# Softmax sums on VectorE in place of ones matmuls, in an attention and FFN block on one core

## The chip, the cores and the metric

The kernel runs on one NeuronCore of one Trainium2 chip. The metric is the device time of one execution in microseconds (us); lower is better.

The engines in question: TensorE (PE in the profile; PEld is its weight load), VectorE (DVE), ScalarE (ACT), and SyncE (SP), whose instruction queue issues nearly all DMA transfers of this kernel. PSUM holds the tiles that TensorE's matmuls write in this kernel (names ending in `_ps`); an "eviction" is the copy or addition by which VectorE or ScalarE empties a PSUM tile.

## The reference, cut to what matters

```python
# x: 1 x 2048 x 1024, 32 query heads of 128, 4 key/value heads, window W = 512, all bf16
mod = (_silu(c) @ w_mod).reshape(c.shape[0], 6, 1, -1)       # sa, ca, ga, sb, cb, gb
h = _layernorm(x) * (1 + ca) + sa
# attention:
q = (x @ wq).reshape(B, Sq, Hq, Dh).transpose(0, 2, 1, 3)    # x is h here
k = jnp.repeat(k_cache[:, :, Sk - W:, :], rep, axis=1)       # v alike
scores = jnp.einsum('bhqd,bhkd->bhqk', q, k) * Dh ** (-0.5)
p = _softmax(scores, axis=-1)
o = jnp.einsum('bhqk,bhkd->bhqd', p, v)
#   ... o @ wo
x = x + ga * attention(h)
h = _layernorm(x) * (1 + cb) + sb
x = x + gb * ((_silu(h @ w_gate) * (h @ w_up)) @ w_down)     # the FFN, 3584 wide
```

The kernel computes `exp(scores)` without subtracting a maximum (it proves a bound on the scores while it runs), so each softmax needs the sum of 512 exponentials per query and head, its reciprocal, and a multiplication of `o` by that reciprocal.

## The kernel before

One step `k` of the attention loop handles one of 128 units: a head of a chunk of 512 tokens, 4 x 32. The exponentials `pT` lie with the keys on the partitions (4 tiles of 128 keys) and the 512 queries along the row. So the sum over keys is a sum over 4 tiles, which VectorE does (`psA`, `psB`), and then a sum over 128 partitions. Before, TensorE did the latter with a matmul against a matrix of ones, once for four heads (`l_ps`), and ScalarE made the reciprocal as `exp(-ln(sum))`. The reciprocals go through DRAM (`r_d`) and come back copied to all partitions (`rb`).

```python
    def mm(name, ...):                        # q_ps, o_ps, a_ps, l_ps share four PSUM tiles
        return psp.tile(list(shape), dt, name=name, tag="mm", bufs=4)
    def fetch(out, in_):                      # every load goes through SyncE, in this order
        pin(nc.sync.dma_start(out=out, in_=in_), "dma")
    ...
    def ln_stats(tt, late=None):              # LayerNorm statistics of 128 tokens
        ...                                   # two bn_stats on VectorE
        nc.vector.bn_aggr(out=mv[:, 0:2], in_=st)
        nc.scalar.activation(out=mv[:, 2:3], in_=mv[:, 1:2], func=ACT.Ln, bias=eps_t)
        nc.scalar.activation(out=mv[:, 2:3], in_=mv[:, 2:3], func=ACT.Exp, scale=-0.5)
    ...
    def put_q(g, q_ps):
        t = wk.tile([P, TCW], BF16, name="qT", tag="row", bufs=5)
        nc.vector.tensor_copy(out=t, in_=q_ps)
    ...
    def emit_s(g):
        ...                                   # 4 s_ps matmuls, 2 exponentials of 128x1024
        nc.vector.tensor_tensor(out=a, in0=p[:, 0:2, :], in1=p[:, 2:4, :], op=ALU.add)   # psA
        b = wk.tile([P, TCW], BF16, name="psB", tag="psB", bufs=5)
        nc.vector.tensor_tensor(out=b, in0=a[:, 0, :], in1=a[:, 1, :], op=ALU.add)
        rec[g] = b

    def emit_l(g):                            # once for four heads
        l_ps = mm("l_ps")
        for i in range(4):
            nc.tensor.matmul(l_ps[32 * i:32 * i + 32, :], lhsT=ones_bf[:, 0:32],
                             rhs=rec.pop(g - 3 + i), start=True, stop=True)
        r = wk.tile([P, TCW], FP32, name="rinv", tag="f32", bufs=2)
        nc.scalar.activation(out=r, in_=l_ps, func=ACT.Ln)
        nc.scalar.activation(out=r, in_=r, func=ACT.Exp, scale=-1.0)
        d = dp.tile([4, TCW], FP32, name="r_d", tag="r_d", bufs=4)
        nc.scalar.dma_start(out=d, in_=r[0:P:32, :])          # written from ScalarE's queue
        rinv[g // 4] = d
    # load_rb: two fetches of r_d, spread to 128 partitions; emit_norm: oT *= rb on VectorE
    ...
    def emit_wo(cc, q, u):                    # output projection: 8 a_ps matmuls, 4 rounds q
        ...
        if q == 0:
            nc.vector.tensor_copy(out=acc[(cc, t)][:, dsl], in_=a_ps)
        elif q < NQ - 1:
            nc.vector.tensor_tensor(out=acc[(cc, t)][:, dsl], in0=a_ps, in1=acc[...], op=ALU.add)
        ...                                   # last round: f, gate, residual
    ...
    for k in range(NU + 1):
        if k % 4 >= 2 and 4 * (k // 4) + 8 < NU:
            g = 4 * (k // 4) + 8
            load_wq(g // H, (g % H) // 4, (k % 4 - 2,))       # one of two tiles of next wq
        if k < NU:
            emit_s(k)
        if k + LEAD < NU:
            emit_q(k + LEAD)                                  # 8 q_ps matmuls, then put_q
        ...
        run_tasks(k)                                          # wo, rb, norm, LayerNorm, loads
        if k >= 1:
            if k % 4 == 0:
                emit_l(k - 1)
            emit_o(k - 1)                                     # 4 o_ps matmuls, copy by ScalarE
```

A scheduler orders the instructions of TensorE, VectorE and ScalarE, apart from those that `pin` keeps in program order. Any edit can therefore shift instructions elsewhere, and single microseconds are approximate.

Of the kernel before, what the change touches and what calls it, by code (L numbers as in the profile page):

```python
# [8 lines left out]
ACT = mybir.ActivationFunctionType  # L9
ALU = mybir.AluOpType  # L10
AX = mybir.AxisListType
BF16 = mybir.dt.bfloat16
FP32 = mybir.dt.float32
# [575 lines left out]
def fast_path(ctx, tc, flag, A_x, A_k_cache, A_v_cache, A_wq, A_wo, B_x, B_w_gate, B_w_up,  # L589
# [3 lines left out]
    nc = tc.nc  # L593
    P = 128
    _, S, D = A_x.shape
# [7 lines left out]
    TCW = 512  # L603
# [9 lines left out]
    scale = float(Dh) ** -0.5  # L613
# [15 lines left out]
    const = ctx.enter_context(tc.tile_pool(name="const", bufs=1))  # L629
# [5 lines left out]
    wk = ctx.enter_context(tc.tile_pool(name="work", bufs=2))  # L635
# [4 lines left out]
    def blkA(name, shape, dt=BF16):  # L640
        return pa_.tile(shape, dt, name=name, tag="A")

    def blkB(name, shape, dt=BF16):
        return pb_.tile(shape, dt, name=name, tag="B")
# [4 lines left out]
    def mm(name, shape=(P, 512), dt=FP32):  # L649
        return psp.tile(list(shape), dt, name=name, tag="mm", bufs=4)  # L650

    def big(name, shape=(P, 2, 512), dt=FP32):
        return psp.tile(list(shape), dt, name=name, tag="s", bufs=2)
# [6 lines left out]
    def pin(ins, what="steps"):  # L660
        return tc.keep_in_program_order(ins) if stage[what] else ins

    def fetch(out, in_):
        pin(nc.sync.dma_start(out=out, in_=in_), "dma")  # L664

    def load(out, in_):
        with nc.allow_non_contiguous_dma(reason="weight slice"):
            fetch(out=out, in_=in_)
# [20 lines left out]
    def load_wq(cc, hg, parts=(0, 1)):  # L689
        for i in parts:  # L690
            t = blkB("wq", [P, 4, 512])
            load(t, wq_v[:, 4 * i:4 * i + 4, hg * 512:(hg + 1) * 512])
            wq_tiles[(cc, hg, i)] = t
# [8 lines left out]
    for kv in range(Hkv):  # L702
        pin(nc.sync.dma_start_transpose(  # L703
            out=kT[:, kv, :], in_=A_k_cache[0, kv, k0:k0 + W, :]), "dma")
# [8 lines left out]
    ones_bf = const.tile([P, P], BF16, name="ones_bf")  # L713
# [13 lines left out]
    warm(16)  # L727
    modT = const.tile([P, 4, DT], FP32, name="modT")
    sa, ca1, sb, cb1 = (modT[:, i, :] for i in range(4))
    ga_bc = const.tile([P, D], FP32, name="ga_bc")  # L730
    gb_bc = const.tile([P, D], FP32, name="gb_bc")


    ec = wk.tile([DT, P], FP32, name="ec", tag="f32", bufs=2)
# [56 lines left out]
    def load_gate(n, k, dst):  # L791
        fetch(out=dst.rearrange("p (a b) -> p a b", a=2),
                          in_=row_d[n][k:k + 2, :].partition_broadcast(P))

    def load_cols(n, k, dst, add_one):
        src = row_d[n][k:k + 2, :].rearrange("a (b p) -> p (a b)", p=P)
        with nc.allow_non_contiguous_dma(reason="1024 values to columns"):
            fetch(out=dst, in_=src)
        if add_one:
            nc.vector.tensor_scalar(out=dst, in0=dst, scalar1=1.0, scalar2=None, op0=ALU.add)  # L800

    tasks = {}

    def at(k, f, *a):
        tasks.setdefault(k, []).append((f, a))
# [18 lines left out]
    def ln_norm(tt, on_act=False):  # L824
        mv = ln.pop(tt)
        n = wk.tile([P, D], BF16, name="xn", tag="xn", bufs=3)
        if on_act:
            nc.vector.scalar_tensor_tensor(out=mv[:, 3:4], in0=mv[:, 0:1], scalar=-1.0,
                                           in1=mv[:, 2:3], op0=ALU.mult, op1=ALU.mult)
            nc.scalar.activation(out=n, in_=xt[tt], func=ACT.Identity, bias=mv[:, 3:4],  # L830
                                 scale=mv[:, 2:3])
        else:
            pin(nc.vector.tensor_scalar(out=n, in0=xt[tt], scalar1=mv[:, 0:1],  # L833
                                        scalar2=mv[:, 2:3], op0=ALU.subtract, op1=ALU.mult))
        return n
# [75 lines left out]

    def put_q(g, q_ps):
        t = wk.tile([P, TCW], BF16, name="qT", tag="row", bufs=5)
        nc.vector.tensor_copy(out=t, in_=q_ps)  # L914
        qT[g] = t


# [3 lines left out]
    for t in range(QT):  # L921
        ln_stats(t)
        n = ln_norm(t, t % 2 == 0)
# [5 lines left out]
    for half in range(DH):  # L929
# [6 lines left out]
        for n in range(4 * LEAD):  # L936
            dt, g = (4 * half + n // LEAD, n % LEAD) if half == 0 else (4 + n % 4, n // 4)
            nc.tensor.matmul(q0_ps[g],
                             lhsT=wq_tiles[(0, 0, dt // 4)][:, dt % 4, g * P:(g + 1) * P],
                             rhs=hT[("h1", 0)][:, dt, :], start=(dt == 0), stop=(dt == DT - 1))  # L940
# [65 lines left out]
    NU = NTC * H  # L1006
    pT = {}
    oT = {}
    rec = {}
    rinv = {}  # L1010
# [13 lines left out]
    def emit_s(g):  # L1024
        kv = (g % H) // rep
        p = blkA("pT", [P, WT, TCW])
        for jj in range(WT // 2):
            s_ps = big("s_ps")
            for i in range(2):
                j = 2 * jj + i  # L1030
                nc.tensor.matmul(s_ps[:, i, :], lhsT=kT[:, kv, j * P:(j + 1) * P], rhs=qT[g],  # L1031
                                 start=True, stop=True)
            nc.scalar.activation(out=p[:, 2 * jj:2 * jj + 2, :], in_=s_ps, func=ACT.Exp,  # L1033
                                 scale=scale)
        del qT[g]
        pT[g] = p
        a = wk.tile([P, 2, TCW], BF16, name="psA", tag="psA", bufs=2)
        nc.vector.tensor_tensor(out=a, in0=p[:, 0:2, :], in1=p[:, 2:4, :], op=ALU.add)  # L1038
        b = wk.tile([P, TCW], BF16, name="psB", tag="psB", bufs=5)
        nc.vector.tensor_tensor(out=b, in0=a[:, 0, :], in1=a[:, 1, :], op=ALU.add)  # L1040
        rec[g] = b

    def emit_l(g):


        l_ps = mm("l_ps")
        for i in range(4):
            nc.tensor.matmul(l_ps[32 * i:32 * i + 32, :], lhsT=ones_bf[:, 0:32],  # L1048
                             rhs=rec.pop(g - 3 + i), start=True, stop=True)
        r = wk.tile([P, TCW], FP32, name="rinv", tag="f32", bufs=2)  # L1050
        nc.scalar.activation(out=r, in_=l_ps, func=ACT.Ln)
        nc.scalar.activation(out=r, in_=r, func=ACT.Exp, scale=-1.0)
        d = dp.tile([4, TCW], FP32, name="r_d", tag="r_d", bufs=4)
        nc.scalar.dma_start(out=d, in_=r[0:P:32, :])
        rinv[g // 4] = d

    def load_rb(g):
# [55 lines left out]
    for n, vecs in enumerate(((2, 4), (5, 3))):  # L1113
        for part in range(2):
            k = 16 * n + 8 * part
            at(k, load_rows, vecs[0], part)
            at(k + 2, load_rows, vecs[1], part)
            at(k + 5, mod_rows, n, part)
        at(16 * n + 15, load_gate, n, 0, gb_bc if n else ga_bc)
        at(16 * n + 16, load_cols, n, 2, sb if n else cb1, n == 0)  # L1120
    for tt in range(QT, S // P):
        cc, t = divmod(tt, QT)
        at(max((cc - 1) * H - 16, 0) + 2 + 2 * t, load_x, tt)
# [7 lines left out]
    at(NU - H + 29, bound_mod)  # L1131
    at(NU + 3, bound_final)
    for g in range(3, NU, 4):
        at(g + 2, load_rb, g)
        at(g + 4, emit_norm, g)
    for cc in range(1, NTC):
# [17 lines left out]
    def load_gu(cc, fg):  # L1154
        for nm, v in (("wg", wg_v), ("wu", wu_v)):
            for i in range(2):
                t = blkB(nm, [P, 4, 512])
                load(t, v[:, 4 * i:4 * i + 4, fg * 512:(fg + 1) * 512])
                gu_w[(cc, fg, nm, i)] = t

# [20 lines left out]
    def emit_down(cc, dh, t, widths=(512,)):  # L1181
        row = (cc * QT + t) * P
        c0 = 0
        for w in widths:
            dsl = slice(dh * 512 + c0, dh * 512 + c0 + w)
            d_ps = mm("d_ps", (P, w))
            for f in range(FT):
                nc.tensor.matmul(d_ps, lhsT=guT[(cc, f // 4)][:, f % 4, t * P:(t + 1) * P],  # L1188
                                 rhs=wd_tiles[(cc, dh, f // 4)][:, f % 4, c0:c0 + w],
                                 start=(f == 0), stop=(f == FT - 1))  # L1190
            r = wk.tile([P, w], FP32, name="f32", tag="f32", bufs=2)
            nc.vector.tensor_tensor(out=r, in0=d_ps, in1=gb_bc[:, dsl], op=ALU.mult)
            o = wk.tile([P, w], BF16, name="o_sb", tag="row", bufs=5)
            nc.vector.tensor_tensor(out=o, in0=r, in1=xt[cc * QT + t][:, dsl], op=ALU.add)
            nc.scalar.dma_start(out=out2d[row:row + P, dsl], in_=o)
            c0 += w
# [6 lines left out]
# [3 lines that stand above are left out]
            load_wq(g // H, (g % H) // 4, (k % 4 - 2,))  # L1206
# [3 lines that stand above are left out]
            emit_q(k + LEAD)  # L1210
        if k == NU - 4:
            load_gu(0, 0)
        run_tasks(k)
        if k >= 1:
            if k % 4 == 0:
                emit_l(k - 1)
            emit_o(k - 1)
    stage.update(dma=False, steps=False)
    for cc in range(NTC):
# [56 lines left out]
```

## Time and profile before

The recorded time is 1293.48 us, the median of 3 runs (1293.3 to 1294.21). Of the profiled run's 1290.1 us span, the attention loop takes the first 680 us and the FFN the rest.

| what | number | view |
|---|---|---|
| TensorE busy | 99% | busy table |
| chain of waits that ended last | 95% TensorE | chain |
| one l_ps group, on TensorE | 0.42 us x 32 | timeline |
| VectorE busy, 30 to 700 us | 486.5 of 670 us | windows |

The busy table (us, share of the span) and the chain that ended last (shares of the span by engine, then by engine and line) of before:

```profile
PE 1271.4 (99%) x6073; PEld 577.4 (45%) x6193; DVE 653.1 (51%) x1159; ACT 433.7 (34%) x625; POOL 1.2 (0%) x7
PE 95%; SPq 2%; DMA 1%; DVE 1%; issue 1%; DVEq 0%
```

TensorE is the limit. The windows view of before (the interval, its length, busy us and count for each engine, granted clock, DMA share, GB/s) shows by how much VectorE is second:

```profile
200.00:300.00 100.00, 99.53 (x466) 44.42 (x473) 83.13 (x148) 53.66 (x81) 0.00 (x0) 1.00 0.66 183
400.00:500.00 100.00, 99.52 (x465) 44.47 (x473) 77.94 (x138) 52.77 (x76) 0.00 (x0) 1.00 0.60 171
500.00:600.00 100.00, 99.47 (x463) 44.59 (x472) 71.58 (x118) 51.18 (x68) 0.00 (x0) 1.00 0.54 166
600.00:700.00 100.00, 99.53 (x466) 44.50 (x474) 69.12 (x153) 49.62 (x70) 0.00 (x0) 1.00 0.60 178
```

The third number is TensorE, the fifth (83.13 in the first line) VectorE, the sixth ScalarE. TensorE hardly stops, and VectorE has 17 to 31 us of slack in each of these 100 us.

The timeline of before around one l_ps group (start, busy us, engine, line, operation) shows what the ones matmuls cost:

```profile
411.41 1.89 PE L1095 MATMUL a_ps<-wo,oT 128*128 128x512 bf16 x8
413.23 0.40 PE L1048 MATMUL l_ps<-psB,ones_bf 128*32 128x512 bf16 x4
413.56 1.04 PE L1079 MATMUL o_ps<-pT,v_sb 128*128 128x512 bf16 x4
```

From a_ps to o_ps takes 2.15 us here and 1.73 us in steps without l_ps. The difference, 0.42 us, times 32 groups is 13.4 us.

Two waits of before matter later (engine, line and tile that waited, for whom: us in total, times, longest):

```profile
ACT mv L820 <- DVE mv L819: 20.8, 14, 3.2
PE gu_ps L1168 <- DMA wu<-in_B_w_up_dram: 1.7, 1, 1.7
```

The first is ScalarE waiting for VectorE's LayerNorm statistics. TensorE's only long wait in the middle of the kernel is near 762 us, for an FFN weight tile.

### The profile page before, as it was taken

The numbers are of one execution on the slowest core, as the hardware profiler recorded it, in microseconds if no ns is written. First come the engines' busy times: TensorE is split into PE (matmuls) and PEld (weight loads), VectorE is DVE, ScalarE is ACT, GpSimd is POOL, SyncE is SP. The second block draws the span as 40 slices with busy tenths as digits, with TensorE's granted clock in tenths as the row PEclk, the third lists the DMA queues.
The fourth block names the chain that finished last, engine by engine and source line by source line (L and its number), as shares of the span: only waits on it lengthen the run. The fifth ranks groups of instructions, "written<-read, shape, count | busy, mean of one in ns | idle before, by whom it ended". The sixth has DMA issues, their size and how long they took to land.

```text
span 1290.1 us, 15319 instructions
## 1 busy us (share of the span) xinstructions
PE 1271.4 (99%) x6073; PEld 577.4 (45%) x6193; DVE 653.1 (51%) x1159; ACT 433.7 (34%) x625; POOL 1.2 (0%) x7
## 2 busy tenths in 40 slices
PE   8999999999999999999999999999999999999998
PEld 4444444444444444444444444444444444444444
DVE  5575668976688867597865641222122111222122
ACT  4755545554555555555552111011100111011100
POOL 0000000000000000000000000000000000000000
PEclk9999999999999999999999999999999999999999
DMA  9788565567365655455657485454536445454402
GB/s 290 242 277 256 178 196 139 170 174 219 103 193 144 189 146 175 146 165 143 185 194 238 127 240 182 136 192 131 171 105 220 157 148 178 135 192 131 147 18 84
DMA packets 219939, 221.08 MB, mean 171 GB/s; under 512 B 45385, under 2 KB 205129, under 8 KB 219858
## 3 DMA queue, kind: packets, MB, share of 16 engines
q1 hardware_dynamic: 214690, 215.54, 54.5%
q10 hardware_dynamic: 5168, 4.46, 1.0%
q8 instruction: 50, 0.82, 0.3%
q14 instruction: 31, 0.25, 0.1%
HBM read 207.63 MB, written 4.47 MB: 164 GB/s over the span
## 4 chain that ended last, share of the span: by engine, by line
PE 95%; SPq 2%; DMA 1%; DVE 1%; issue 1%; DVEq 0%
PE gu_ps L1168 29%; PE a_ps L1095 17%; PE q_ps L1018 17%; PE d_ps L1188 15%; PE o_ps L1079 9%; PE s_ps L1031 8%; SPq L664 1%; PE l_ps L1048 1%; SPq L703 1%; DMA hT<-xn 0%; DMA wq<-in_A_wq_dram 0%; DMA wu<-in_B_w_up_dram 0%; PE row_ps L777 0%; DVE guT L1174 0%; DVE xn L833 0%
## 5 line engine op out<-in xcount | busy, mean ns | idle before, releaser
L1033 ACT ACTIVATE pT<-s_ps 128x1024 bf16<-128x1024 f32 x256 | 252.0, 1026 | 72.8 <-PE s_ps L1031 67.3
L1095 PE MATMUL a_ps<-wo,oT 128*128 128x512 bf16 x972 | 238.9, 379 | 2.6
L1018 PE MATMUL q_ps<-hT,wq 128*128 128x512 bf16 x994 | 236.1, 379 | 0.8 <-DVE modT L753 0.3
L1173 ACT ACTIVATE sg<-gu_ps 128x512 bf16<-128x512 f32 x112 | 66.9, 597 | 486.0 <-PE gu_ps L1168 420.4
L1174 DVE TENSOR_TENSOR guT<-gu_ps,sg 128x512 bf16<-128x512 f32 x112 | 77.4, 691 | 280.0 <-ACT sg L1173 280.0
L1168 PE MATMUL gu_ps<-hT,wu 128*128 128x512 bf16 x878 | 210.1, 379 | 2.6 <-DMA wu<-in_B_w_up_dram 1.7
L1168 PE MATMUL gu_ps<-hT,wg 128*128 128x512 bf16 x877 | 210.0, 379 | 1.1
L1188 PE MATMUL d_ps<-wd,guT 128*128 128x512 bf16 (+2 forms) x934 | 193.2, 366 | 0.9
L1095 PEld LDWEIGHTS <-oT 128*128 128x128 bf16 x1024 | 100.0, 98 | 121.4 <-issue 1.3
L1018 PEld LDWEIGHTS <-wq 128*128 128x128 bf16 x1000 | 97.8, 98 | 118.5 <-DMA wq<-in_A_wq_dram 0.7
L1188 PEld LDWEIGHTS <-guT 128*128 128x128 bf16 x952 | 90.9, 98 | 103.0
L1168 PEld LDWEIGHTS <-wu 128*128 128x128 bf16 x896 | 87.6, 98 | 107.8 <-DMA wu<-in_B_w_up_dram 2.2
L1168 PEld LDWEIGHTS <-wg 128*128 128x128 bf16 x896 | 87.7, 98 | 105.7
L1038 DVE TENSOR_TENSOR psA<-pT 128x1024 bf16<-128x1024 bf16 x128 | 87.8, 686 | 89.0 <-ACT pT L1033 88.9
L1031 PE MATMUL s_ps<-qT,kT 128*128 128x512 bf16 x508 | 131.1, 379 | 0.7 <-ACT pT L1033 0.6
L1079 PE MATMUL o_ps<-pT,v_sb 128*128 128x512 bf16 x510 | 131.5, 380 | 0.2
L1081 ACT CAST oT<-o_ps 128x512 bf16<-128x512 f32 x128 | 74.5, 582 | 166.4 <-PE o_ps L1079 166.4
L914 DVE CAST qT<-q_ps 128x512 bf16<-128x512 f32 x128 | 87.5, 685 | 78.6 <-PE q_ps L1018 77.9
L1031 PEld LDWEIGHTS <-kT 128*128 128x128 bf16 x512 | 50.1, 98 | 61.5 <-issue 1.5
L1069 DVE TENSOR_TENSOR oT<-oT,rb 128x1024 bf16<-128x1024 bf16 x64 | 75.4, 1218 | 1.5 <-DMA rb<-r_d 1.5
L1079 PEld LDWEIGHTS <-v_sb 128*128 128x128 bf16 x512 | 47.4, 98 | 60.3 <-issue 7.7
L1040 DVE TENSOR_TENSOR psB<-psA 128x512 bf16<-128x512 bf16 x128 | 53.4, 417 | 0.6
(279 smaller groups left out, 443.2 us busy)
## 6 DMA issues: line engine op xcount, KB each, us to landing
wq<-in_A_wq_dram SPq DMA_DIRECT2D x64, 512.0 KB
rb<-r_d SPq DMA_DIRECT2D x64, 512.0 KB
wo<-in_A_wo_dram SPq DMA_DIRECT2D x64, 512.0 KB
wg<-in_B_w_gate_dram SPq DMA_DIRECT2D x56, 512.0 KB
wu<-in_B_w_up_dram SPq DMA_DIRECT2D x56, 512.0 KB
wd<-in_B_w_down_dram SPq DMA_DIRECT2D x56, 512.0 KB
wmr<-in_w_mod_dram SPq DMA_DIRECT2D x8, 1024.0 KB
out_dram<-o_sb ACTq DMA_DIRECT2D x31, 128.0 KB
```

The source lines that it names most:

```text
L914: nc.vector.tensor_copy(out=t, in_=q_ps)
L1018: nc.tensor.matmul(q_ps, lhsT=wq_tiles[(cc, h // 4, dt // 4)][:, dt % 4, (h % 4) * P:(h % 4 + 1) * P], rhs=hT[("h1", cc)][:, dt, :], start ...
L1031: nc.tensor.matmul(s_ps[:, i, :], lhsT=kT[:, kv, j * P:(j + 1) * P], rhs=qT[g], start=True, stop=True)
L1033: nc.scalar.activation(out=p[:, 2 * jj:2 * jj + 2, :], in_=s_ps, func=ACT.Exp, scale=scale)
L1038: nc.vector.tensor_tensor(out=a, in0=p[:, 0:2, :], in1=p[:, 2:4, :], op=ALU.add)
L1069: pin(nc.vector.tensor_tensor(out=oo, in0=oo, in1=rb, op=ALU.mult))
L1079: nc.tensor.matmul(o_ps, lhsT=v_sb[:, kv, j, :], rhs=pT[g][:, j, :], start=(j == 0), stop=(j == WT - 1))
L1081: nc.scalar.copy(out=oT[(cc, hg)][:, hi, :], in_=o_ps)
L1095: nc.tensor.matmul(a_ps, lhsT=oT[(cc, 2 * q + i)][:, hh % 4, t * P:(t + 1) * P], rhs=wo_tiles[(cc, q, dh, i)][:, hh % 4, :], start=(hh == ...
L1168: nc.tensor.matmul(ps[:, n, :], lhsT=gu_w[(cc, fg, nm, dt // 4)][:, dt % 4, fi * P:(fi + 1) * P], rhs=hT[("h2", cc)][:, dt, :], start=(dt ...
L1174: nc.vector.tensor_tensor(out=guT[(cc, fg)][:, fi, :], in0=ps[:, 1, :], in1=g, op=ALU.mult)
L1188: nc.tensor.matmul(d_ps, lhsT=guT[(cc, f // 4)][:, f % 4, t * P:(t + 1) * P], rhs=wd_tiles[(cc, dh, f // 4)][:, f % 4, c0:c0 + w], start=( ...
```

## The change

The intent: take the l_ps matmuls off TensorE, the limiting engine. As the program lays it out, VectorE transposes `psB` in 32x32 blocks, which brings 32 keys onto each row, sums the rows, folds the four partition groups of 32 with two copies and two additions, takes the reciprocal and transposes it back. To make room, ScalarE copies q out of PSUM instead of VectorE. A second, separate part gives the fourth FFN weight tile its own double buffer, in space that frees up. The diff, cut to its core:

```diff
 def put_q(g, q_ps):
-    nc.vector.tensor_copy(out=t, in_=q_ps)
+    nc.scalar.copy(out=t, in_=q_ps)
 # emit_s, after psB
-    rec[g] = b
+    t = wk.tile([P, TCW // 32, 32], BF16, name="psT", tag="psT", bufs=2)
+    nc.vector.transpose(out=t.rearrange("p b k -> p (b k)"), in_=b)
+    if g % 4 == 0:
+        rec[g // 4] = wk.tile([P, 4, TCW // 32], FP32, name="psR", tag="psR", bufs=2)
+    nc.vector.tensor_reduce(out=rec[g // 4][:, g % 4, :], in_=t, axis=AX.X, op=ALU.add)
 def emit_l(g):
-    l_ps = mm("l_ps")
-    for i in range(4):
-        nc.tensor.matmul(l_ps[32 * i:32 * i + 32, :], lhsT=ones_bf[:, 0:32], ...)
-    nc.scalar.activation(out=r, in_=l_ps, func=ACT.Ln)
-    nc.scalar.activation(out=r, in_=r, func=ACT.Exp, scale=-1.0)
-    nc.scalar.dma_start(out=d, in_=r[0:P:32, :])
+    r = rec.pop(g // 4).rearrange("p h b -> p (h b)")
+    for n in (64, 32):
+        nc.vector.tensor_copy(out=c[0:n, :], in_=r[n:2 * n, :])
+        nc.vector.tensor_tensor(out=r[0:n, :], in0=r[0:n, :], in1=c[0:n, :], op=ALU.add)
+    nc.vector.reciprocal(out=r[0:32, :], in_=r[0:32, :])
+    nc.vector.transpose(out=t.rearrange("c j q -> c (j q)"), in_=r[0:32, :])
+    fetch(out=d.rearrange("(j h) (b q) -> (h b) j q", h=2, q=32), in_=t)   # SyncE's queue
 # load_gu, the FFN's weights
+    if nm == "wu" and i == 1:
+        t = wk.tile([P, 4, 512], BF16, name=nm, tag="rb", bufs=2)
 # the rest: emit_l becomes a task, psB has 2 buffers instead of 5, the second gate's tile moves
 # (no run tests these alone)
```

The write of `r_d` now goes through SyncE's queue, ahead of later weight loads. And `rinv` now comes from VectorE instead of ScalarE.

More of the change, by code (lines that the diff above doesn't have):

```diff
@@ L729, in fast_path @@
     sa, ca1, sb, cb1 = (modT[:, i, :] for i in range(4))
-    ga_bc = const.tile([P, D], FP32, name="ga_bc")
-    gb_bc = const.tile([P, D], FP32, name="gb_bc")
+    ga_bc = const.tile([P, D], FP32, name="ga_bc", tag="gate")
     ec = wk.tile([DT, P], FP32, name="ec", tag="f32", bufs=2)
@@ L800, in load_cols, with gate_b @@
             nc.vector.tensor_scalar(out=dst, in0=dst, scalar1=1.0, scalar2=None, op0=ALU.add)
+    gates = []
+    def gate_b():
+        gates.append(const.tile([P, D], FP32, name="gb_bc", tag="gate"))
+        load_gate(1, 0, gates[0])
     tasks = {}
@@ L1038, in emit_s @@
         nc.vector.tensor_tensor(out=a, in0=p[:, 0:2, :], in1=p[:, 2:4, :], op=ALU.add)
-        b = wk.tile([P, TCW], BF16, name="psB", tag="psB", bufs=5)
+        b = wk.tile([P, TCW], BF16, name="psB", tag="psB", bufs=2)
         nc.vector.tensor_tensor(out=b, in0=a[:, 0, :], in1=a[:, 1, :], op=ALU.add)
-        rec[g] = b
-    def emit_l(g):
-        l_ps = mm("l_ps")
-        for i in range(4):
-            nc.tensor.matmul(l_ps[32 * i:32 * i + 32, :], lhsT=ones_bf[:, 0:32],
-                             rhs=rec.pop(g - 3 + i), start=True, stop=True)
-        r = wk.tile([P, TCW], FP32, name="rinv", tag="f32", bufs=2)
-        nc.scalar.activation(out=r, in_=l_ps, func=ACT.Ln)
-        nc.scalar.activation(out=r, in_=r, func=ACT.Exp, scale=-1.0)
+        t = wk.tile([P, TCW // 32, 32], BF16, name="psT", tag="psT", bufs=2)
[3 more added lines that the diff above has]
+        nc.vector.tensor_reduce(out=rec[g // 4][:, g % 4, :], in_=t, axis=AX.X, op=ALU.add)
+    def emit_l(g):
+        r = rec.pop(g // 4).rearrange("p h b -> p (h b)")
+        c = wk.tile([64, 64], FP32, name="fold", tag="fold", bufs=2)
+        for n in (64, 32):
+            nc.vector.tensor_copy(out=c[0:n, :], in_=r[n:2 * n, :])
+            nc.vector.tensor_tensor(out=r[0:n, :], in0=r[0:n, :], in1=c[0:n, :], op=ALU.add)
+        nc.vector.reciprocal(out=r[0:32, :], in_=r[0:32, :])
+        t = wk.tile([32, 2, 32], FP32, name="rinv", tag="rinv", bufs=2)
+        nc.vector.transpose(out=t.rearrange("c j q -> c (j q)"), in_=r[0:32, :])
         d = dp.tile([4, TCW], FP32, name="r_d", tag="r_d", bufs=4)
-        nc.scalar.dma_start(out=d, in_=r[0:P:32, :])
+        fetch(out=d.rearrange("(j h) (b q) -> (h b) j q", h=2, q=32), in_=t)
         rinv[g // 4] = d
@@ L1118, in fast_path @@
             at(k + 5, mod_rows, n, part)
-        at(16 * n + 15, load_gate, n, 0, gb_bc if n else ga_bc)
         at(16 * n + 16, load_cols, n, 2, sb if n else cb1, n == 0)
+    at(15, load_gate, 0, 0, ga_bc)
+    at(NU + 16, gate_b)
     for tt in range(QT, S // P):
@@ L1133, in fast_path @@
     for g in range(3, NU, 4):
+        at(g + 1, emit_l, g)
         at(g + 2, load_rb, g)
@@ L1156, in load_gu @@
             for i in range(2):
-                t = blkB(nm, [P, 4, 512])
+                if nm == "wu" and i == 1:
+                    t = wk.tile([P, 4, 512], BF16, name=nm, tag="rb", bufs=2)
+                else:
+                    t = blkB(nm, [P, 4, 512])
                 load(t, v[:, 4 * i:4 * i + 4, fg * 512:(fg + 1) * 512])
@@ L1191, in emit_down @@
             r = wk.tile([P, w], FP32, name="f32", tag="f32", bufs=2)
-            nc.vector.tensor_tensor(out=r, in0=d_ps, in1=gb_bc[:, dsl], op=ALU.mult)
+            nc.vector.tensor_tensor(out=r, in0=d_ps, in1=gates[0][:, dsl], op=ALU.mult)
             o = wk.tile([P, w], BF16, name="o_sb", tag="row", bufs=5)
@@ L1214, in fast_path @@
         if k >= 1:
-            if k % 4 == 0:
-                emit_l(k - 1)
             emit_o(k - 1)
```

## The prediction

> **What bounds the kernel now.** TensorE. The page's busy table gives PE 1271.4 of 1290.1 us (99%), the chain of waits is 95% PE, and the granted clock is 0.98 to 1.00 in every window. A full attention step (8 q, 8 a, 4 o, 4 s matmuls) takes 5.18 us in the timeline. VectorE is second, only in the attention stage: between 42 and 680 us the windows show DVE 470.7 of 638.6 us busy (15.2 us per 20.6 us group of four heads), single groups 18 to 20.4 us. ACT has 343.8 there.
>
> **Removed.** The 32 l_ps groups. In the timeline, from an a_ps group to the next o_ps group takes 2.15 us with l_ps and 1.73 without: 0.42 us each, 13.4 us in all, on the PE chain. Also ACT's Ln and Exp of them (39.3 us, off the chain), and DVE's q copies (128 x 685 ns; 0.60 us start to start).
>
> **Moved.** q copies to ACT (about 0.58 us each, like the o copy): harmless. r_d's write goes to the SP queue, where it waits for VectorE and holds back later loads.
>
> **Added on DVE.** Per head a 128x512 bf16 transpose and a 512-wide row sum. [...] This trace has neither operation[...]. Estimate: 2 x 0.72 - 0.60 = 0.84 us more per head. Per group of four: two copies, two adds, a small transpose at about 0.2 us each, and a reciprocal (64 elements; the 128-element one took 923 ns, so about 0.54): about 1.7 us. Sum: 5.1 us per group, so DVE rises from 15.2 to about 20.3 us per group, against a PE group of about 20.2 without l_ps. DVE is as full as PE on average and overfull in the groups with wo's last additions, LayerNorm and weight-norm checks (207 to 300, 350 to 454, 557 to 640 us). Adding 5.1 us to each window leaves some 32 us above PE's 20.2; backlog that slack groups drain takes back perhaps 12.
>
> **FFN weights.** The chain shows one wait for wu (1.75 us of PE at 760 us); double buffering saves 2 to 4 us.
>
> **Sum.** 1293.5 - 13.4 + 20 - 2.5 = about 1297 us. Range 1281 to 1316. Chances: faster by over 2% 0.02, within 2% 0.90, slower by over 2% 0.08.
>
> **What would show it.** No l_ps group, and the a-to-o step back at 1.73 us. Transpose and row sum near 0.7 us each. DVE over 95% busy in 207 to 300 and 350 to 454 us. PE busy under 98% there, with idle before a_ps, o_ps or q_ps released by DVE (evictions of a_ps, normalization of oT). FFN from 800 us unchanged; the wu wait near 760 gone. Normalization waiting for rb more than the present 1.5 us, since r_d is written later.
>
> **What would make it wrong.** Transpose or row sum [...]overlapping better than assumed: then DVE has slack, PE keeps its pace, and 1278 to 1282 us results. Or the other way: [...]SP's wait for r_d delaying wo and wq loads; then 1315 or more.

The 0.72 us for each of the two new operations was the author's estimate. It carries over what other VectorE operations on 512 elements show in the trace of before: three f32 operations in a row took 0.69 us each and started at 744.16, 744.88 and 745.61 us, 0.72 to 0.73 us apart. That the new operations would be as slow was not shown then.

## The result, and the profile after

After took 1306.27 us (median of 4 runs, 1302.21 to 1306.93), before 1293.74 us in the same rounds (1293.3 to 1294.21). The ratio is 1.0090, with a 95% interval of 1.0069 to 1.0111. Ratios here are the mean time of one kernel's runs over the mean of the other's runs in the same rounds, so they are not quite the ratio of the medians quoted. The kernel is slower by about 0.9%, or 12 us. The experiments ran on several chips, so kernels are compared below by their ratio to before.

The busy table and the chain of after:

```profile
PE 1273.4 (98%) x6065; PEld 576.7 (44%) x6065; DVE 780.2 (60%) x1479; ACT 467.6 (36%) x689; POOL 1.2 (0%) x7
PE 67%; DVE 24%; DMA 5%; ACT 2%; issue 1%; SPq 1%; DVEq 0%
```

VectorE's busy time rose by 127.1 us, and 24% of the chain that ended last now runs through VectorE, against 1% before. The costliest groups of after (busy us, mean ns of one, idle before and its main releaser) show what was added, and where TensorE now waits:

```profile
L1106 PE MATMUL a_ps<-wo,oT 128*128 128x512 bf16 x1024 | 245.5, 383 | 6.2 <-DVE acc L1112 3.4
L1023 PE MATMUL q_ps<-hT,wq 128*128 128x512 bf16 x1000 | 238.3, 379 | 9.0 <-DMA wq<-in_A_wq_dram 6.7
L1048 DVE STREAM_TRANSPOSE psT<-psB 128x512 bf16<-128x512 bf16 x128 | 90.1, 704 | 2.5
L1051 DVE TENSOR_REDUCE psR<-psT 128x16 f32<-128x512 bf16 x128 | 86.9, 679 | 2.5
```

The transpose takes 704 ns and the row sum 679 ns, as estimated. TensorE idles before a_ps, for VectorE's evictions, and before q_ps, for the weights wq. The same windows of after:

```profile
200.00:300.00 100.00, 96.04 (x436) 42.74 (x435) 96.95 (x188) 56.15 (x86) 0.00 (x0) 0.98 0.57 159
400.00:500.00 100.00, 95.54 (x438) 42.28 (x437) 95.49 (x187) 56.20 (x84) 0.00 (x0) 1.00 0.67 170
500.00:600.00 100.00, 100.00 (x465) 45.28 (x464) 91.61 (x169) 57.20 (x77) 0.00 (x0) 1.00 0.44 138
600.00:700.00 100.00, 93.41 (x421) 41.38 (x419) 90.13 (x207) 53.10 (x77) 0.00 (x0) 0.98 0.63 185
```

The third line is instructive: with VectorE 91.6% busy, TensorE lost nothing. In the last line VectorE is less busy, 90.1%, and TensorE is idle for 6.6 us. But that window mixes two stages: 3.7 of the 6.6 us fall between 680 and 700 us, where q_ps has run out, so that a step gives TensorE less work and VectorE as much as before. A cleaner pair of windows lies inside the full loop:

```profile
560.00:600.00 40.00, 40.00 (x187) 18.10 (x186) 39.54 (x74) 23.42 (x31) 0.00 (x0) 1.00 0.31 104
640.00:660.00 20.00, 18.54 (x86) 8.20 (x85) 16.32 (x41) 11.41 (x16) 0.00 (x0) 1.00 0.66 172
```

VectorE is 99% busy in the first and TensorE loses nothing; it is 82% busy in the second and TensorE loses 1.46 us. So the load of a window alone does not set the loss in that window. This does not exclude a backlog that was built up in one window and paid for in a later one; e10 below speaks to that.

**A ledger of TensorE.** In a full stream, matmuls of 512 columns start 0.2155 us apart in these traces. I counted every stop between 30 and 800 us: the time beyond 0.2155 us from one start to the next wherever the trace shows TensorE idle for more than 0.1 us. Before has 2.5 us of such stops. After has 25.0 us in 24 stops: 12.0 us for evictions by VectorE, 7.8 for wq, 2.9 for exponentials by ScalarE, 2.3 for other tiles. Another 3.9 us went to matmuls that ran 0.427 us apart, half speed, behind the three stops of 2.1 to 2.8 us that end at 74.8, 263.3 and 692.1 us (the granted clock is 0.50 from 75.6 to 78.9, 263.4 to 266.6 and 693.5 to 696.7 us). The stop of 1.62 us that ends at 784.30 was followed by eight matmuls in 1.89 us, full speed. Saved 13.4, lost 25.0 + 3.9 - 2.5 = 26.4: the ledger says +13.0 us, and the profiled spans differ by 1304.4 - 1290.1 = 14.3. (The profiled execution of before took 1291.92 us, 1.6 less than the median of its timed runs.) So the expected gain was delivered, and a larger loss came with it.

The timeline of after shows one such stop, with VectorE, ScalarE and TensorE together (a bracket is the idle time before the instruction, and its releaser):

```profile
260.70 1.28 DVE L819 BATCH_NORM_STATS2 st<-x_91 128x6 f32<-128x512 bf16 x2
261.89 0.68 DVE L1043 TENSOR_TENSOR psA<-pT 128x1024 bf16<-128x1024 bf16 x1
262.49 0.20 DVE L824 BATCH_NORM_AGGREGATE mv<-st 128x2 f32<-128x12 f32 x1
262.61 0.64 DVE L1112 COPY acc<-a_ps 128x512 f32<-128x512 f32 x1
262.72 0.29 ACT L825 ACTIVATE mv<-mv,eps_t 128x1 f32<-128x1 f32 x1 [3.36 <-DVE mv L824]
262.93 0.57 ACT L1092 CAST oT<-o_ps 128x512 bf16<-128x512 f32 x1
263.30 3.55 PE L1106 MATMUL a_ps<-wo,oT 128*128 128x512 bf16 x8 [2.23 <-DVE acc L1112]
```

VectorE is working without a break. Because it is late, ScalarE sits idle for 3.36 us in front of a LayerNorm step of 0.29 us, with two o copies, an exponential and a q copy queued behind it. TensorE waits 2.23 us for a PSUM tile. Then its eight a_ps matmuls take 3.55 us instead of 1.89: the clock had dropped (the windows view has a granted clock of 0.50 from 264 to 266 us).

Nothing overtook the LayerNorm step in ScalarE's queue here: the o copy of 262.93 needs nothing from VectorE, and the four o_ps matmuls that it copies had run from 251.67 to 252.70, but it starts 0.21 us after the LayerNorm step. From start to start, matmuls of this trace are 427 ns apart in the slow stretch and 215.5 ns in a full stream.

A second path is SyncE's queue. The timeline of after, SyncE only, and then the matmuls that wait:

```profile
300.06 0.33 SPq L664 DMA_DIRECT2D r_d<-rinv  x1
300.49 0.38 SPq L664 DMA_DIRECT2D wo<-in_A_wo_dram  x1
301.46 0.81 SPq L664 DMA_DIRECT2D rb<-r_d  x2
302.37 2.59 SPq L851 DMA_TRANSPOSE hT<-xn  x1
305.42 1.22 SPq L664 DMA_DIRECT2D wo<-in_A_wo_dram  x1
306.70 1.30 SPq L664 DMA_DIRECT2D wq<-in_A_wq_dram  x1
...
310.45 0.44 SPq L664 DMA_DIRECT2D wq<-in_A_wq_dram  x1
...
317.23 1.04 PE L1023 MATMUL q_ps<-hT,wq 128*128 128x512 bf16 x4 [1.14 <-DMA wq<-in_A_wq_dram]
```

The write r_d can start only when VectorE has finished rinv (its transpose ran from 299.8 to 300.0). What stands behind it in the queue starts after it, up to the second wq tile at 310.45, which TensorE could have used from 316.1 (317.23 less the 1.14 us of idle time).

The waits of after that answer to those shown of before, and SyncE's own:

```profile
ACT mv L825 <- DVE mv L824: 48.2, 24, 3.6
SPq L664 <- DVE rinv L1063: 173.8, 15, 19.3
PE gu_ps L1184 <- DVE guT L1190: 1.6, 1, 1.6
```

ScalarE's wait for LayerNorm statistics more than doubled, from 20.8 to 48.2 us. SyncE waits for VectorE's rinv. The FFN's wait for wu is gone, and one of the same size, for guT, has come in its place.

### The profile page after: what moved, and what is told of

Its sections match the earlier page's. It is cut to its first block, busy times and chain, and to the rows that moved or that the text cites. A ratio compares the mean times of both kernels' runs of the same rounds, so it can differ in the third digit from the quotient of the medians. Undisturbed runs are those within 1.5% of the kernel's fastest.

```text
span 1304.4 us, 15495 instructions
## 1 busy us (share of the span) xinstructions
PE 1273.4 (98%) x6065; PEld 576.7 (44%) x6065; DVE 780.2 (60%) x1479; ACT 467.6 (36%) x689; POOL 1.2 (0%) x7
## 4 chain that ended last, share of the span: by engine, by line
PE 67%; DVE 24%; DMA 5%; ACT 2%; issue 1%; SPq 1%; DVEq 0%
PE gu_ps L1184 29%; PE d_ps L1204 15%; PE a_ps L1106 8%; PE q_ps L1023 7%; PE o_ps L1090 3%; PE s_ps L1036 3%; DVE psT L1048 3%; DVE psA L1043 3%; DVE psR L1051 3%; DVE oT L1080 3%; DVE junk L958 2%; DMA wq<-in_A_wq_dram 2%; DVE psB L1045 2%; DVE st L819 2%; ACT pT L1038 1%; DMA hT<-xn 1%
## 5 line engine op out<-in xcount | busy, mean ns | idle before, releaser
L1106 PE MATMUL a_ps<-wo,oT 128*128 128x512 bf16 x1024 | 245.5, 383 | 6.2 <-DVE acc L1112 3.4
L1184 PE MATMUL gu_ps<-hT,wg 128*128 128x512 bf16 x896 | 213.2, 381 | 1.6 <-DVE guT L1190 1.6
L1106 PEld LDWEIGHTS <-oT 128*128 128x128 bf16 x1024 | 100.3, 98 | 130.3 <-issue 11.2
L1048 DVE STREAM_TRANSPOSE psT<-psB 128x512 bf16<-128x512 bf16 x128 | 90.1, 704 | 2.5
L1051 DVE TENSOR_REDUCE psR<-psT 128x16 f32<-128x512 bf16 x128 | 86.9, 679 | 2.5
L919 ACT CAST qT<-q_ps 128x512 bf16<-128x512 f32 x128 | 75.2, 589 | 36.1 <-PE q_ps L1023 34.9
```

Source lines behind the costliest of these rows:

```text
L919: nc.scalar.copy(out=t, in_=q_ps)
L1048: nc.vector.transpose(out=t.rearrange("p b k -> p (b k)"), in_=b)
L1051: nc.vector.tensor_reduce(out=rec[g // 4][:, g % 4, :], in_=t, axis=AX.X, op=ALU.add)
L1106: nc.tensor.matmul(a_ps, lhsT=oT[(cc, 2 * q + i)][:, hh % 4, t * P:(t + 1) * P], rhs=wo_tiles[(cc, q, dh, i)][:, hh % 4, :], start=(hh == ...
L1184: nc.tensor.matmul(ps[:, n, :], lhsT=gu_w[(cc, fg, nm, dt // 4)][:, dt % 4, fi * P:(fi + 1) * P], rhs=hT[("h2", cc)][:, dt, :], start=(dt ...
```

## The experiments

**Theory.** The loss comes from VectorE being late, and instructions that wait for it pass its lateness on to those queued behind them, which need nothing from VectorE: on SyncE from r_d to wq, on ScalarE from the LayerNorm step to the copies and exponentials, and on VectorE from the new work to the evictions. **Rivals.** VectorE simply lacks throughput, so only its total work counts; or q copies on ScalarE do the harm; or the FFN buffer does.

The comparison with the reference is weak for this change: even e9, which is wrong, passes. The layouts of after and of e11 (which e12 shares), followed index by index, do give each query its own sum, and e9's does not.

The ledger for the kernels without l_ps, with the measure defined above. "Ledger" is -13.4 + stops + half speed - 2.5; "span" is the profiled span minus 1290.1. Both are in us. "Evictions by VectorE" are the waits for acc, f and, in e2, qT. Each row is one execution, and e6's is the fastest of its four (1297.85 to 1304.58 us), so its row flatters it.

| kernel | ratio to before | stops: wq | evictions by VectorE | ScalarE | other | half speed | ledger | span |
|---|---|---|---|---|---|---|---|---|
| after | 1.0090 | 7.8 | 12.0 | 2.9 | 2.3 | 3.9 | +13.0 | +14.3 |
| e1 r_d, rb on GpSimd's queue | 1.0010 | 0 | 0.7 | 11.2 | 5.1 | 0 | +1.1 | +2.5 |
| e2 q copy on VectorE | 1.0322 | 8.9 | 33.3 | 6.7 | 1.5 | 3.9 | +38.4 | +44.1 |
| e3 wq norms on ScalarE | 1.0117 | 3.7 | 6.3 | 14.5 | 3.2 | 3.2 | +15.0 | +16.1 |
| e5 LayerNorm step later | 1.0022 | 10.1 | 5.7 | 1.5 | 2.9 | 0.6 | +4.9 | +6.5 |
| e6 wq loads ahead of r_d | 1.0064 | 0 | 13.3 | 3.3 | 3.6 | 1.5 | +5.9 | +6.0 |
| e7 e1 and e5 | 1.0035 | 0 | 5.8 | 5.0 | 6.7 | 1.7 | +3.3 | +4.3 |
| e9 no transpose | 0.9951 | 1.5 | 3.3 | 2.2 | 3.3 | 0 | -5.7 | -5.6 |
| e10 e5 and e6 | 0.9999 | 0 | 6.4 | 2.8 | 4.6 | 1.3 | -0.8 | -0.2 |
| e11 e10, 32-bit transpose | 0.9957 | 0 | 7.1 | 0 | 3.1 | 1.5 | -4.2 | -3.8 |
| e12 e11, first acc copy on ScalarE | 0.9921 | 0 | 1.1 | 0 | 3.8 | 0 | -11.0 | -10.2 |

The ledger meets the span within 1.6 us in every row but e2's (5.7 off). That is the support for reading the time from TensorE's stops at all. What a kernel loses is its ledger entry plus 13.4: 26.4 us in after, 14.5 in e1, 12.6 in e10, 7.7 in e9, 2.4 in e12.

### e1: r_d and rb through GpSimd's queue

```diff
-    fetch(out=d.rearrange(...), in_=t)
+    nc.gpsimd.dma_start(out=d.rearrange(...), in_=t)
-    fetch(out=rb, in_=d[2 * i:2 * i + 2, :].partition_broadcast(P))
+    nc.gpsimd.dma_start(out=rb, in_=d[2 * i:2 * i + 2, :].partition_broadcast(P))
```

> The changed kernel with the row-sum write r_d and the two rb loads issued by GpSimd's queue instead of SyncE's, so that SyncE no longer waits for VectorE's rinv before it issues wq and wo loads; VectorE's work is unchanged. Trace of the changed kernel: TensorE lost about 7.8 us waiting for wq, plus about 1.7 us at half rate after the longest of these waits, and about 15 us for evictions of a_ps by VectorE. Theory A (the queue behind r_d is a cost of its own): the wq waits fall from 6.7 us to under 1 us and the time falls by 7 to 10 us, to about 1297 to 1299. Rival B (all of it is VectorE's load; a wait for wq only replaces a wait for VectorE): wq waits vanish but the time stays within 3 us of 1306.

Measured: 1293.85 us against 1292.71, ratio 1.0010 (0.9982 to 1.0038). That is faster than the theory expected (1297 to 1299). VectorE's work is as large as in after (779.9 us busy in the whole run, against 780.2), yet nearly all of the slowdown against before is gone: 14.5 us are lost where after loses 26.4. The stops for wq went from 7.8 us to none. The evictions' stops fell too, from 12.0 to 0.7 us. Other waits grew; the waits view of e1:

```profile
ACT mv L825 <- DVE mv L824: 68.6, 26, 5.8
PE s_ps L1036 <- ACT pT L1038: 9.5, 14, 1.4
```

ScalarE waits for LayerNorm even longer, and TensorE now waits for ScalarE's exponentials. What follows: with the same work on VectorE, the queue that carries r_d and rb decides nearly half of the loss. How much of e1's gain is wq's and how much is other loads being earlier and instructions falling differently, this run does not separate.

### e2: the q copy back on VectorE

```diff
-        nc.scalar.copy(out=t, in_=q_ps)
+        nc.vector.tensor_copy(out=t, in_=q_ps)
```

> The changed kernel with the q copies back on VectorE. If VectorE's load is what costs (theory: it stood at 92 to 97% busy between 200 and 700 us), 128 x 0.60 us = 77 us more work finds almost no room there: the attention stage grows by 45 to 75 us, to about 1350 to 1380 us, with VectorE over 98% busy. Rival (stalls come from waits and queue order, VectorE still has slack): under 15 us more.

Measured: 1335.83 us, ratio 1.0322 (1.0295 to 1.0350), slower by over 2%. That is less than the theory expected (1350 to 1380) and more than its rival did (under 15 us above after). More work on VectorE brings far more stops: 33.3 us for evictions, 19.7 of them for the q copies themselves. Moving q to ScalarE was necessary for the change, not its fault.

### e3: the weight norms on ScalarE

```diff
-        pin(nc.vector.scalar_tensor_tensor(out=junk, in0=w, scalar=1.0, in1=w, op0=ALU.mult,
-                                           op1=ALU.mult, accum_out=sq[:, col:col + 1]))
+        nc.scalar.activation(out=junk, in_=w, func=ACT.Square, accum_out=sq[:, col:col + 1])
```

> The changed kernel with the 32 squared-norm sums of wq moved from VectorE (38.6 us of 1.21 us each) to ScalarE. VectorE is relieved by 39 us or 6% of its attention load, most of it in its fullest groups; ScalarE gets about 33 to 40 us. If VectorE's load is the cause, evictions and rinv come earlier, both kinds of TensorE waits shrink by half or more and the time falls by 12 to 20 us, to about 1286 to 1294. Rival (queue order of loads, or ScalarE's q copies in front of its exponentials, are the cause): within 4 us of 1306, or slower.

Measured: 1308.40 us, ratio 1.0117 (1.0091 to 1.0143), no better than after: the expected 12 to 20 us did not come. VectorE lost work (580.3 us busy between 30 and 700 us, against 609.2), and the stops for its evictions fell from 12.0 to 6.3 us and for wq from 7.8 to 3.7. But the stops for ScalarE rose from 2.9 to 14.5 us. The waits of e3 show why:

```profile
ACT mv L825 <- DVE mv L824: 29.7, 19, 3.4
ACT junk L958 <- DMA wq<-in_A_wq_dram: 27.3, 8, 6.0
```

ScalarE waited less for LayerNorm than in after (48.2 us), but 27.3 us for wq tiles in front of the moved norms (junk). The edit also dropped the `pin` and gave junk a buffer of its own, and the scheduler put the norms earlier (the first at 154.7 us instead of 184.4), eight of them before their tile had landed. Of the 14.5 us of stops, 11.6 come within 8 us after such a wait. So the moved work held up ScalarE's queue itself. The run shows that relief of VectorE can be lost in another engine's queue; it is no clean test of the rival "only VectorE's total counts", because it added a new wait. e10 is the better one.

### e4: before, with only the q copy on ScalarE

```diff
-        nc.vector.tensor_copy(out=t, in_=q_ps)
+        nc.scalar.copy(out=t, in_=q_ps)
```

> The kernel before with only the q copies moved to ScalarE. VectorE goes down by 77 us, ScalarE up by 75 us. TensorE was never held by VectorE in the kernel before, so the move alone should change nothing: 1292 to 1295 us. If ScalarE's q copies delay its exponentials (rival for part of the loss, 3.4 us of waits for pT in the changed kernel), 3 to 5 us slower.

Measured: 1294.10 us against 1292.71, ratio 1.0007 (0.9978 to 1.0036). TensorE's stops between 30 and 800 us are 2.8 us, against 2.5. The interval of the times is wide (-2.8 to +4.7 us), so it is the stops that decide. This part of the change is harmless by itself, and brings nothing either.

### e5: the LayerNorm step of ScalarE later

```diff
-        nc.vector.bn_aggr(out=mv[:, 0:2], in_=st)
-        nc.scalar.activation(out=mv[:, 2:3], in_=mv[:, 1:2], func=ACT.Ln, bias=eps_t)
-        nc.scalar.activation(out=mv[:, 2:3], in_=mv[:, 2:3], func=ACT.Exp, scale=-0.5)
+        pin(nc.vector.bn_aggr(out=mv[:, 0:2], in_=st))
+    def ln_rstd(tt):            # called after emit_o of the next step
+        mv = ln[tt]
+        pin(nc.scalar.activation(out=mv[:, 2:3], in_=mv[:, 1:2], func=ACT.Ln, bias=eps_t))
+        nc.scalar.activation(out=mv[:, 2:3], in_=mv[:, 2:3], func=ACT.Exp, scale=-0.5)
 # ln_rows and ln_xpose follow one step later
```

> The changed kernel with LayerNorm's two tiny ScalarE operations (mv: Ln and Exp of one column) issued after the next step's o copy instead of at once, and its normalization and transpose one step later. In the changed kernel ScalarE sat idle 48.2 us (24 times, up to 3.6) in front of the Ln, waiting for VectorE's bn_aggr, with exponentials and copies queued behind it; before: 20.8 us. VectorE's and ScalarE's work is unchanged. Theory C (the in-order ScalarE queue hands VectorE's lateness to TensorE at this place): the waits for mv fall below 15 us, the stops of TensorE near 259 to 263 and 613 us go, and the time falls by 4 to 9 us, to 1297 to 1302. Rival: waits for mv were harmless; within 3 us of 1306.

(What the trace of after shows of ScalarE's queue is the stop at 262.72 us above: 3.36 us of idle time, with o copies behind it whose matmuls were over.)

Measured: 1296.95 us against 1293.45, ratio 1.0022 (1.0004 to 1.0040), clear of after's interval and at the edge of the expected 1297 to 1302. No operation is added or taken away. The waits of e5:

```profile
ACT mv L832 <- DVE mv L825: 15.3, 8, 3.9
PE q_ps L1030 <- DMA wq<-in_A_wq_dram: 8.8, 8, 2.9
```

ScalarE's wait for LayerNorm fell from 48.2 to 15.3 us, and the stops for VectorE's evictions from 12.0 to 5.7. The wq waits stayed, as they should: they belong to the other path. That the evictions gain because ScalarE, being earlier, hands its exponentials to VectorE earlier is an argument, and no run shows it alone.

### e6: both wq loads ahead of r_d in SyncE's queue

```diff
-        if k % 4 >= 2 and 4 * (k // 4) + 8 < NU:
-            g = 4 * (k // 4) + 8
-            load_wq(g // H, (g % H) // 4, (k % 4 - 2,))
 # the first norms of wq (bound_wq) come up to three steps earlier
 # after emit_q, ahead of run_tasks
+        if k % 4 == 0 and k + 8 < NU:
+            load_wq((k + 8) // H, ((k + 8) % H) // 4)
```

> The changed kernel with r_d and rb still on SyncE's queue, but the two wq loads of a group put in front of that group's r_d write instead of behind it and the rb loads. VectorE's load is unchanged, GpSimd stays idle. Theory A (wq loads come late because they stand behind a write that waits for VectorE): TensorE's waits for wq fall from 6.7 us to under 1 us, and the time falls by 6 to 10 us, to 1296 to 1300. Rival (e1 was faster for another reason, another order of instructions or a second queue): within 3 us of 1306.

Measured: 1300.49 us against 1293.45, ratio 1.0064 (1.0043 to 1.0084). That is half a microsecond above the expected range. The wq stops are gone (7.8 to 0). The interval overlaps after's, so the gain of about 0.3% is not resolved by the times alone. The loads are also issued two and three steps earlier than in after, so the run does not separate being earlier from standing ahead of r_d. The evictions and the LayerNorm waits (52.7 us, against 48.2) stayed as they were.

### e7: e1 and e5 together

```diff
+        nc.gpsimd.dma_start(...)        # r_d and rb, as in e1
+        ln_rstd(tt)                     # after emit_o, as in e5
```

> Both: r_d and rb on GpSimd's queue (e1, 1293.9) and LayerNorm's ScalarE operations later (e5). e1's trace left 9.5 us of TensorE waiting for pT, each time with ScalarE idle up to 5.8 us for mv in front. Theory A with C: those waits go too, 1283 to 1287, clear of the kernel before (1292.7). If VectorE's fullness is the floor: no gain over e1, 1292 to 1295.

Measured: 1297.09 us, ratio 1.0035 (1.0016 to 1.0054). This is a miss: no better than e5 and no better than e1. ScalarE still waited 36.8 us for LayerNorm, and VectorE waited 13.9 us for rb (2.3 in after), as it did in e1 (14.7). Why the two gains do not add up is left open. The rb tiles landing later through GpSimd's queue is one candidate.

### e8: before, with only the fourth FFN tile double buffered

```diff
-                t = blkB(nm, [P, 4, 512])
+                if nm == "wu" and i == 1:
+                    t = wk.tile([P, 4, 512], BF16, name=nm, tag="rb", bufs=2)
+                else:
+                    t = blkB(nm, [P, 4, 512])
```

> The kernel before with the fourth FFN tile double buffered, and nothing else. If the wait for wu near 760 us (1.75 us of TensorE) is removed: 1.5 to 2.5 us faster. If the next thing that ends there takes its place (the transposes of hT and the affine of the last chunk, as guT does in the changed kernel: 1.6 us), under 0.7 us of change.

Measured over 5 rounds: 1292.23 us against 1293.45, ratio 0.9992 (0.9978 to 1.0006). The wu wait is gone and a guT stop of 0.9 us has come; the time is not resolved from zero (-2.8 to +0.8 us). The FFN part did not make the 12 us.

### e9: after without the transposes (wrong on purpose)

```diff
-        nc.vector.transpose(out=t.rearrange("p b k -> p (b k)"), in_=b)
-        nc.vector.tensor_reduce(out=rec[g // 4][:, g % 4, :], in_=t, axis=AX.X, op=ALU.add)
+        nc.vector.tensor_reduce(out=rec[g // 4][:, g % 4, :],
+                                in_=b.rearrange("p (b k) -> p b k", k=32), axis=AX.X, op=ALU.add)
```

> The changed kernel without the 128 big transposes: each row sum reads psB itself. The result is wrong on purpose; every queue, buffer and copy is left. VectorE is relieved by 90 us. In e5, e6 and e1 VectorE's load was the same as in the changed kernel and the time fell by 6 to 12 us, so this asks for the root. Theory D (the places where TensorE stops all hand on VectorE's lateness): rinv, bn_aggr and evictions come early again, all three kinds of TensorE waits fall to under 5 us in sum and the time shows the saved matmuls, 1279 to 1284. Rival (queue order itself costs, whatever VectorE's load; e3 relieved it by 39 us for nothing): 1293 or more.

Measured: 1286.14 us against 1293.21, ratio 0.9951 (0.9933 to 0.9970). Every queue is as in after, only the 90 us of transposes are gone (VectorE's busy time, in which overlapping instructions count once, fell from 780.2 to 705.3), and the stops on both large paths shrink together: for evictions from 12.0 to 3.3 us, for wq from 7.8 to 1.5. So VectorE's added work is the root, and the queues are the way it reaches TensorE. The two findings do not contradict each other. The time missed the expected 1279 to 1284, and the three kinds of waits sum to 7.0 us, not under 5; the rival (1293 or more) is out.

### e10: e5 and e6 together

```diff
+        ln_rstd(tt)                     # after emit_o, as in e5
+            load_wq((k + 8) // H, ((k + 8) % H) // 4)      # ahead of run_tasks, as in e6
```

> The changed kernel with e5 and e6 together: LayerNorm's ScalarE operations later and the wq loads in front of r_d. e5 left 10 us of wq waits, e6 left 13 us of evictions and 3.3 of pT. If the two are separate outlets: 1287 to 1292, a little below the kernel before. If e7's disappointment repeats (a stop removed reappears elsewhere because VectorE is as late as ever): 1295 to 1299.

Measured: 1293.09 us against 1293.21, ratio 0.9999 (0.9984 to 1.0015). The expected 1287 to 1292 is missed by 1 us. With the same operations as after, in another order, the slowdown against before is gone: VectorE is busy 778.3 us in the whole run, after 780.2, and TensorE's stops fell from 25.0 to 13.8 us. So the rival "only VectorE's total counts" fails. But 12.6 of the 26.4 us lost remain, and they pay back what the l_ps groups saved; they shrink further when VectorE has less to do (9.2 us in e11, 2.4 in e12). No run reorders something harmless as a control, so part of the gain could come from the scheduler laying out other instructions differently; that the waits aimed at fell (wq to none, LayerNorm from 48.2 to 19.2 us) speaks against it.

### e11: e10 with 32-bit transposes

```diff
-        t = wk.tile([P, TCW // 32, 32], BF16, name="psT", tag="psT", bufs=2)
-        nc.vector.transpose(out=t.rearrange("p b k -> p (b k)"), in_=b)
+        t = wk.tile([P, TCW // 2], FP32, name="psT", tag="psT", bufs=2)
+        nc.vector.transpose(out=t, in_=b.bitcast(FP32))
-        nc.vector.tensor_reduce(out=rec[g // 4][:, g % 4, :], in_=t, ...)
+        nc.vector.tensor_reduce(out=rec[g // 4][:, g % 4, :].rearrange("p (b t) -> p b t", t=2),
+                in_=t.bitcast(BF16).rearrange("p (b k t) -> p b t k", k=32, t=2), ...)
 # emit_norm reads rb in the order that results
+            oo = oo.rearrange("p h (b c t) -> p (h b) c t", c=32, t=2)
+            rv = rb.rearrange("p h (b t c) -> p (h b) c t", c=32, t=2)
```

Two neighbouring bf16 sums are moved as one 32-bit element. The sums then come out with even and odd queries apart, and the normalization reads rb in that order.

> e10 with the transposes done on pairs: psB read as 256 32-bit values per row, so that a block transpose moves two bf16 at once; the row sum picks the pairs apart and the normalization reads rb in the permuted order. A correct result is meant. [...]the transpose falls from 0.70 to about 0.42 us and VectorE from about 92% to 87% of the attention stage: 1283 to 1289, faster than both kernels. [...]

(The rival was no gain over e10. The 0.42 us was the author's estimate, which no trace showed. Two transposes of after lead to nearly the same, again as an estimate: 64 elements (rinv, 32-bit) took 0.22 us and 512 (psT, bf16) 0.70, and a straight line between them gives 0.43 us at 256.)

Measured over 5 rounds: 1288.11 us against 1293.21, ratio 0.9957 (0.9943 to 0.9970): it beats both kernels, by less than 2%. Here is the transpose's group in e11 (duration ns min, median and max):

```profile
L1055 DVE STREAM_TRANSPOSE psT<-psB x128: 395/445/448, 30.2 to 675.6; 128x256 f32<-128x256 f32 x128
```

It takes 445 ns, against 704 in after. The row sum is unchanged (median 686 ns).

### e12: e11 with the first acc copy on ScalarE

```diff
-            nc.vector.tensor_copy(out=acc[(cc, t)][:, dsl], in_=a_ps)
+            nc.scalar.copy(out=acc[(cc, t)][:, dsl], in_=a_ps)
```

> The kernel is e11_pair with one more edit: the first eviction of every acc tile (the copy of a_ps into acc, 32 x 2 of them) runs on ScalarE. In e11 TensorE still stops 7.1 us for evictions of acc by VectorE, out of 10.2 us of stops in all. Theory: what is left is VectorE's lateness at those evictions, ScalarE has room there and q, o copies already come from it, so the acc stops fall below 4 us, no new ScalarE stop over 2 us appears, and the time is 1283 to 1287. Rival, after e3: work moved to ScalarE comes back as waits of TensorE for ScalarE (pT, oT, qT evictions), because ScalarE's queue has waits of its own; then acc stops fall but stops released by ACT grow by as much, and the time is 1288 or more.

(There are 32 such copies, of 585 ns each by the trace; the text miscounts them.) Measured over 5 rounds: 1281.96 us against 1293.02, ratio 0.9921 (0.9907 to 0.9934). That is faster than the theory's own range, though also within 2%. The eviction stops fell from 7.1 to 1.1 us, and no stop for ScalarE appeared. The chain of e12:

```profile
PE 92%; DMA 3%; DVE 3%; ACT 1%; issue 1%; SPq 0%; DVEq 0%
```

TensorE is the limit again, and of the 13.4 us that the l_ps groups cost, the profiled span keeps 10.2. Compare e3: there the moved work waited in ScalarE's queue, up to 6.0 us for a weight tile. The copies moved here wait for TensorE's own a_ps (27.9 us in 28 waits, 1.1 at the longest; two more waits, 4.2 us, have no named releaser), and no stop of TensorE follows. That the LayerNorm wait had been moved first may have helped; no run has these copies on ScalarE without it.

## Why the prediction was right or wrong

The time, 1306.27 us, lies in the range (1281 to 1316) and "within 2%" was the likely one, but the centre was low: +3.5 us predicted, about +12 measured. The range is wide enough to hold before's own time, so hitting it says little; the terms below say more.

1. *TensorE is the limit and an l_ps group costs 0.42 us, 13.4 in all.* Right. The ledger needs the whole 13.4 to close, with and without large losses (e2 apart), and e12 keeps 10.2 of it.
2. *Transpose and row sum at about 0.7 us each.* Right: 704 and 679 ns. The row sum took about as long as the f32 additions into acc, which also have 512 elements (673 ns in after).
3. *VectorE gains 5.1 us per group of four heads.* Too high: 127.1 us of busy time over 32 groups are 4.0. From start to start, as the estimate counts, the traces give about 4.2: a transpose 0.70, a row sum 0.60 (0.72 was assumed), the q copy 0.60 less, and 1.4 for the small operations of a group (1.7 was assumed; one by one, the copies take 0.19 us, the additions 0.21, the reciprocal 0.53 and the small transpose 0.22).
4. *VectorE over 95% busy from 207 to 300 and from 350 to 454 us.* Right: 90.11 of 93 us and 101.46 of 104.
5. *Its fullness costs 20 us: 32 us of work above TensorE's pace, less 12 that slack groups drain.* This is the term that failed, and 6.4 of the 9 us by which the centre was low (the other 2.5 are in 8). It measured 26.4 us of stops and half-speed matmuls (25.0 + 3.9 - 2.5). That 20 came so near is partly luck: the waits it had in mind, for VectorE's evictions, measured 12.0 us, and the rest came by paths to which it gave no number. A comparison of busy sums of two engines explains at most about half of the loss: with after's own operations in another order (e10), 13.8 of the 26.4 us disappear. For that half, what counted was when VectorE finished the few instructions that others queue behind. The other 12.6 us stayed.
6. *"r_d's write goes to the SP queue, where it waits for VectorE and holds back later loads."* The mechanism was right, was named, and was given no number; it was kept as a cause for 1315 us or more. It belonged into the sum: SyncE waited 173.8 us for rinv in after, and 7.8 us of TensorE's stops are waits for wq, and e1 and e6 take them all away (what that alone is worth in time is not resolved, see e6). The ScalarE path, where e5 shows about 9 us (1.0090 to 1.0022), was not foreseen.
7. *q copies on ScalarE are harmless.* Right (e4), and necessary (e2).
8. *FFN double buffering saves 2.5 us.* Not seen: the wu wait of 1.9 us went away, a stop of 1.8 us for guT came, and alone (e8) the change is resolved neither from zero nor from 2.5 us. From the first to the last d_ps matmul, both kernels take 483.6 us.
9. *Normalization waits longer for rb.* Hardly: 2.3 us against 1.5.

## What to carry to other kernels

When you move work from the limiting engine to one that is already 70 to 80% busy, don't only compare busy sums: list every instruction of other engines and every queued DMA that waits for the receiving engine, and ask what stands behind each of them in its queue. Put such waiting instructions behind the urgent ones (later LayerNorm step, earlier weight loads), then cheapen the added work, then spread it. Before moving work to another engine, ask what it will wait for there: moving the norms to ScalarE was useless, because they waited for weights in its queue (e3), and moving acc copies was worth 0.4% (e11 to e12). That these steps have to come in this order is not shown.
